# From which slice on a second weight-conversion step is allowed: slice 18 or slice 13

## The chip, the cores and the metric

One core of a Trainium2 chip runs the whole program. The metric is the device time of one execution in microseconds (us). TensorE does the matrix products (PE in the profile, PEld its weight loads), VectorE is DVE, ScalarE ACT, GpSimd POOL, and SyncE (SP) issues most DMAs.

## The reference

Three layers follow each other:

```
attn: q, k, v of (4 batches, 8 heads, 576, 64); heads 0-3 masked to a band of 32, heads 4-7 to a stride of 32
x = attn as (2304 tokens, 512)
h = x @ w_in                      # 512 -> 2048
x = (h * sigmoid(1.702 h)) @ w_out  # 2048 -> 512
logits = x @ w_gate + log1p(exp(x @ w_noise)) * noise   # 8 experts, best two of each token
out[token] += weight * (relu(x @ w1[e]) @ w2[e])        # 512 -> 1024 -> 512
```

All is in float32. The part that the change touches is the second layer, the two products with `w_in` and `w_out`.

## The kernel before, in words

The second layer works on 6 chunks of 384 tokens, and its 2048 hidden columns are cut into 16 weight slices of 128. A step of the main loop is one (chunk, slice) pair, and here it is called a slice and numbered by its place `i` in the list `seq`: slices 0 to 7 are the first half of chunk 0, slices 8 to 23 the sixteen of chunk 1 (the "second chunk"), slices 24 to 31 the second half of chunk 0, then chunks 2 to 5. So the weight slices 8 to 15 are used for the first time in slices 16 to 23.

For accuracy each float32 operand is held as a rounded `hi` part and a remainder `lo`, and each product is made of three: hi by hi, hi by lo, lo by hi. In slice i TensorE runs the first product of slice i (`m1_l1`, lines 426 to 428, twelve matmuls) and then the second product of slice i-1 (`m1_l2`, lines 450 to 452, nine matmuls). Between a slice's two products lies the activation: ACT's tanh (L431), DVE's L433, ACT's rounding to the hi part of g (L438), and DVE's subtraction to the lo part (L440). L450 and L451 read g's hi part, L452 its lo part; L450 and L452 read the hi part of the weights, L451 their lo part.

The weights come as int64 words that hold two float32 numbers, and must be converted first. A wide piece is half a weight slice, 512 columns (`area`), for weight slices 0 to 13; the last two slices come in narrow pieces of 256 columns (`raw`). Each weight slice's half 0 goes to the first product, half 1 to the second. A conversion step (`w_step`, `w_bits`) takes one wide piece or up to two narrow ones, with three operations on DVE for each piece (L387, L390, L394). A generator yields between them, so that the loop strews them among the other DVE work. Half a slice later `w_split` emits the piece's rounding on ACT (L361) and its remainder on POOL (L362), and issues the load of the next piece into the buffer that this frees. Four wide pieces are under way at any time, and two narrow ones; a narrow piece may be stepped only `LATE = 2` calls of `w_split` (one slice) after its load was issued.

Every slice has one step in its first half, beside its first product: L387 is then ahead of L433 in DVE's order, L390 and L394 between L433 and L440. The first chunk's slices with even i, and all slices from `SMALLS` on, have a second step, behind L440:

```
conv = w_step() if i < HALFC and not i % 2 or i >= SMALLS else iter(())
```

The orders of TensorE, ACT, DVE and POOL are as written out in the program up to the end of chunk 4 (`fine.close()`); after that only TensorE's order is, and the compiler's planner orders the others, as it does SP's queue all the time. Instructions of one engine start in order. The weight loads are chained to each other on SP's queue by `chained`.

Of the kernel before, what the change touches and what calls it, by code (L numbers as in the profile page):

```python
# [52 lines left out]
LATE = 2  # L53
REM = 1
HALFC = NFC // 2
SMALLS = 18
CONVAT = (4, 6, 8, 10, 12, 14)
WAIT1 = 15
R_PP = R_LG + 16 * TPC
# [40 lines left out]
def tile_kernel(ctx, tc, qkL, qkS, vL, vS, wm1, wm2, wgn, noise, cst, lst0, out):  # L100
# [19 lines left out]
    with ExitStack() as main, tc.manual_schedule(engines={mybir.EngineType.PE}):  # L120
# [236 lines left out]
        def w_split():  # L357

            for fc, s, w32, o, n in SPLIT.pop(0):
                hi, lo = W1[fc, s]  # L360
                nc.scalar.copy(hi[:, o:o + n], w32)  # L361
                nc.gpsimd.tensor_sub(lo[:, o:o + n], w32, hi[:, o:o + n].bitcast(F32))  # L362
                if n < 512:
                    held.pop()
                else:
                    w_raw(fc + 2, s)
            w_small()
            SPLIT.append([])
            done.append(0)

        def w_step():
            left = 512
            while PIECES and left:
                fc, s, raw, o, n = PIECES[0]
                if n < 512:
                    if len(done) < born[0] + LATE:
                        return
                    born.pop(0)
                PIECES.pop(0)
                left -= n  # L380
                yield from w_bits(fc, s, raw, o, n)
# [402 lines left out]
        for i, (c, fc) in enumerate(seq):  # L784
# [20 lines left out]
            w_split()  # L805
            conv = w_step() if i < HALFC and not i % 2 or i >= SMALLS else iter(())
            att.norms(conv)
# [219 lines left out]
```

## Time and profile before

| what | value |
|---|---|
| time, median of 3 runs | 1026.28 us (1025.94 to 1031.31) |
| the profiled execution's own time | 1025.36 us |
| its span, first to last instruction | 1023.6 us |
| TensorE busy | 991.5 us, 97% of the span |
| DVE / ACT / POOL busy | 48% / 39% / 22% |
| mean granted TensorE clock | 0.989 |

The profile is one execution on the chip. A busy time is the sum of an engine's instructions; in the timelines each row is one instruction or a run of equal ones, with its start, its duration, the engine, the line of the kernel, the operation, the tile written and the tiles read, and in brackets how long the engine was idle before it and what ended that. A releaser is inferred from semaphores. A matmul's end is modelled, so that consecutive ones overlap in the rows.

### The profile page before, as it was taken

To read this page: it belongs to the slowest core of one execution; us is meant where nothing else is said; L and a number is where in the kernel's file an instruction comes from. 1 tells how busy PE (TensorE), PEld (TensorE's weight loads), DVE (VectorE), ACT (ScalarE), POOL (GpSimd) and SP (SyncE) were. 2 spreads that over 40 slices of the span, in tenths; PEclk is the share of its full clock that TensorE was granted. 3 is DMA by queue.
4 is the path that set the end of the run, shared out by engine and by line. 5 is a ranking of instruction groups with operands and counts; after the bars stand their busy time and mean duration, and the time that the engine had idled before them with its cause. 6 is when DMAs were issued, how large, how long until landed. Compare 5 with 4: busy or idle time off the path is not lost. (4 is left out here: it accounts for less than half of the span.)

```text
span 1023.6 us, 16148 instructions
## 1 busy us (share of the span) xinstructions
PE 991.5 (97%) x5804; PEld 879.8 (86%) x5804; DVE 487.5 (48%) x1520; ACT 394.6 (39%) x1075; POOL 220.2 (22%) x206
## 2 busy tenths in 40 slices
PE   6899999999999999999999999999999999999996
PEld 5778898998888888899988889989999999999995
DVE  6979864547445544523655353342434243333310
ACT  5665533244444444323443242232424233332311
POOL 3565221112000200200320412050322205040303
PEclk9799999999999999999999999999999999999999
DMA  8835512022231325301342255262533527263403
GB/s 290 288 116 179 192 62 72 1 79 44 52 96 55 73 84 192 116 1 63 66 162 73 43 154 124 72 146 103 124 124 90 158 75 173 65 147 118 83 1 52
DMA packets 63393, 107.69 MB, mean 105 GB/s; under 512 B 12096, under 2 KB 25536, under 8 KB 63296
## 3 DMA queue, kind: packets, MB, share of 16 engines
q1 hardware_dynamic: 53104, 85.63, 26.5%
q0 software_dynamic: 10208, 21.02, 10.7%
q8 instruction: 46, 0.75, 0.3%
q14 instruction: 35, 0.29, 0.1%
HBM read 84.04 MB, written 22.73 MB: 104 GB/s over the span
## 5 line engine op out<-in xcount | busy, mean ns | idle before, releaser
L672 DVE SCALAR_TENSOR_TENSOR ht<-pb,ht 128x384 fp32r<-128x384 f32 (+1 forms) x128 | 62.5, 489 | 252.1 <-ACT ht L671 252.1
L671 ACT ACTIVATE ht<-pb 128x384 fp32r<-128x384 f32 (+1 forms) x128 | 56.0, 438 | 260.2 <-PE pb L670 259.2
L426 PE MATMUL pb<-xt,w 128*128 128x384 f32 x384 | 134.9, 351 | 0.0
L428 PE MATMUL pb<-xt,w 128*128 128x384 f32 x384 | 129.6, 337 | 0.0
L427 PE MATMUL pb<-xt,w 128*128 128x384 f32 x384 | 129.5, 337 | 0.0
L702 POOL DMA_INDIRECT out<-y,ix x40 | 64.9, 1623 | 295.0 <-ACT y L701 261.7
L685 PE MATMUL pb<-w,ht 128*128 128x512 f32 x320 | 127.8, 399 | 0.0
L686 PE MATMUL pb<-w,ht 128*128 128x512 f32 x320 | 125.4, 392 | 0.0
L687 PE MATMUL pb<-w,ht 128*128 128x512 f32 x320 | 125.2, 391 | 0.0
L450 PE MATMUL pb<-w,g 128*128 128x512 f32 x288 | 118.3, 411 | 1.8 <-ACT g L438 0.9
L433 DVE SCALAR_TENSOR_TENSOR th<-th,pb 128x384 f32<-128x384 f32 x96 | 53.0, 552 | 128.7 <-ACT th L431 128.6
L451 PE MATMUL pb<-w,g 128*128 128x512 f32 x288 | 113.4, 394 | 0.8 <-POOL w L362 0.8
L452 PE MATMUL pb<-w,g 128*128 128x512 f32 x288 | 114.0, 396 | 0.1
L575 POOL DMA_INDIRECT lst<-pay,si x36 | 36.0, 1001 | 342.6 <-DVE si L572 290.5
L593 DVE TENSOR_TENSOR w<-raw,w 128x512 fp32r<-128x512 f32 x128 | 83.8, 689 | 17.5 <-ACT w L592 17.5
L431 ACT ACTIVATE th<-pb 128x384 f32<-128x384 f32 x96 | 46.9, 489 | 111.4 <-PE pb L428 107.9
L668 PE MATMUL pb<-xa,w 128*128 128x384 f32 x256 | 87.3, 341 | 0.0
L670 PE MATMUL pb<-xa,w 128*128 128x384 f32 x256 | 86.4, 338 | 0.0
L669 PE MATMUL pb<-xa,w 128*128 128x384 f32 x256 | 86.0, 336 | 0.0
L592 ACT CAST w<-raw 128x512 fp32r<-128x512 f32 x128 | 73.8, 618 | 17.2 <-DMA raw<-wm 12.9
L438 ACT CAST g<-th 128x384 fp32r<-128x384 f32 x96 | 49.3, 513 | 75.9 <-DVE th L433 75.9
L426 PEld LDWEIGHTS pb<-xt,w 128*128 128x128 f32 x384 | 72.6, 189 | 2.5
(175 smaller groups left out, 1968.3 us busy)
## 6 DMA issues: line engine op xcount, KB each, us to landing
raw<-wm SPq DMA_DIRECT2D x136, 256.0 KB, 3.0
area<-wm SPq DMA_DIRECT2D x28, 512.0 KB, 4.3
out<-zero SPq DMA_DIRECT2D x7, 768.0 KB, 6.9
qk<-qkL SPq DMA_DIRECT2D x16, 304.0 KB, 3.4
att<-qkS SPq DMA_DIRECT2D x20, 189.0 KB, 4.9
qk<-qkS SPq DMA_DIRECT2D x20, 189.0 KB, 2.6
v<-vL SPq DMA_DIRECT2D x16, 192.0 KB, 3.1
att<-qkL SPq DMA_DIRECT2D x8, 304.0 KB, 6.0
```

The source lines that it names most:

```text
L426: nc.tensor.matmul(ps, w[0][:, a], X[c][:, 0, kc, :], start=(kc == 0), stop=False)
L427: nc.tensor.matmul(ps, w[0][:, a], X[c][:, 1, kc, :], start=False, stop=False)
L428: nc.tensor.matmul(ps, w[1][:, a], X[c][:, 0, kc, :], start=False, stop=(kc == 3))
L450: nc.tensor.matmul(o, g[:, 0, a], w[0], start=((c, fc) in FIRST), stop=False)
L451: nc.tensor.matmul(o, g[:, 0, a], w[1], start=False, stop=False)
L452: m = nc.tensor.matmul(o, g[:, 1, a], w[0], start=False, stop=((c, fc) in LAST))
L668: nc.tensor.matmul(ps, w[:, 0, a], x[:, 0, kc, :], start=(kc == 0), stop=False)
L669: nc.tensor.matmul(ps, w[:, 0, a], x[:, 1, kc, :], start=False, stop=False)
L670: nc.tensor.matmul(ps, w[:, 1, a], x[:, 0, kc, :], start=False, stop=(kc == 3))
L685: nc.tensor.matmul(o, g[:, 0, a], w[:, 0, 512:], start=(fc == 0), stop=False)
L686: nc.tensor.matmul(o, g[:, 0, a], w[:, 1, 512:], start=False, stop=False)
L687: m = nc.tensor.matmul(o, g[:, 1, a], w[:, 0, 512:], start=False, stop=(fc == NF2 - 1))
```

## The change

The constant `SMALLS` goes from 18 to 13. The line quoted above then allows a second step in slices 13 to 17 too: the sixth to the tenth slice of the second chunk. Nothing else changes.

```diff
-SMALLS = 18
+SMALLS = 13
```

## Rows read from the trace of the kernel before

**Rows 1.** The page's first part: busy us, share of the span, number of instructions.
```profile
PE 991.5 (97%) x5804; PEld 879.8 (86%) x5804; DVE 487.5 (48%) x1520; ACT 394.6 (39%) x1075; POOL 220.2 (22%) x206
```

**Rows 2.** Table by stretches, 150 to 200 us: length, busy by engine, clock, DMA.
```profile
150.00:200.00 50.00, 48.43 (x258) 43.10 (x257) 25.13 (x79) 15.76 (x36) 5.20 (x7) 1.00 0.15 47
```

**Rows 3.** Timeline of PE around slice 23's second product.
```profile
171.55 0.50 PE L450 MATMUL pb<-w,g 128*128 128x512 f32 x1 [0.81 <-ACT w L361]
172.81 0.50 PE L451 MATMUL pb<-w,g 128*128 128x512 f32 x1 [0.75 <-POOL w L362]
```

**Rows 4.** Timeline of DVE, 127 to 134 us: end of slice 13, slice 14, start of 15.
```profile
127.06 0.42 DVE L387 TENSOR_SCALAR cv<-area 128x512 int32<-128x512 int32 x1
129.33 0.56 DVE L433 SCALAR_TENSOR_TENSOR th<-th,pb 128x384 f32<-128x384 f32 x1 [1.85 <-ACT th L431]
129.81 0.68 DVE L390 SCALAR_TENSOR_TENSOR cv<-area,cv 128x512 int32<-128x512 int32 x1
130.59 0.69 DVE L394 SCALAR_TENSOR_TENSOR area<-area,cv 128x512 int32<-128x512 int32 x1
131.20 0.55 DVE L440 TENSOR_TENSOR g<-th,g 128x384 fp32r<-128x384 f32 x1
131.67 0.42 DVE L387 TENSOR_SCALAR cv<-area 128x512 int32<-128x512 int32 x1
133.52 0.56 DVE L433 SCALAR_TENSOR_TENSOR th<-th,pb 128x384 f32<-128x384 f32 x1 [1.43 <-ACT th L431]
```

**Rows 5.** Timeline of PE: first L450 and first L452 of slice 14's second product.
```profile
132.80 0.39 PE L450 MATMUL pb<-w,g 128*128 128x512 f32 x1
...
133.26 0.40 PE L452 MATMUL pb<-w,g 128*128 128x512 f32 x1
```

**Rows 6.** Timeline of POOL and ACT, 127 to 132 us.
```profile
127.42 1.28 POOL L362 TENSOR_TENSOR w<-area,w 128x512 fp32r<-128x512 f32 x1 [3.21 <-ACT w L361]
129.92 0.52 ACT L438 CAST g<-th 128x384 fp32r<-128x384 f32 x1 [0.62 <-DVE th L433]
131.32 0.62 ACT L361 CAST w<-area 128x512 fp32r<-128x512 f32 x1 [0.88 <-DVE area L394]
```

**Rows 7.** The page's DMA issues: the wide pieces, KB each, median us to landing.
```profile
area<-wm SPq DMA_DIRECT2D x28, 512.0 KB, 4.3
```

**Rows 8.** Timeline of DVE, a wide step's first two operations in slice 4.
```profile
78.18 0.43 DVE L387 TENSOR_SCALAR cv<-area 128x512 int32<-128x512 int32 x1
...
78.64 0.69 DVE L390 SCALAR_TENSOR_TENSOR cv<-area,cv 128x512 int32<-128x512 int32 x1
```

**Rows 9.** Timeline of POOL and DVE, 95 to 104 us.
```profile
95.77 3.17 POOL L362 TENSOR_TENSOR w<-area,w 128x512 fp32r<-128x512 f32 x2
98.17 1.32 DVE L390 SCALAR_TENSOR_TENSOR cv<-area,cv 128x512 int32<-128x512 int32 x1
...
102.44 1.28 POOL L362 TENSOR_TENSOR w<-area,w 128x512 fp32r<-128x512 f32 x1 [3.50 <-ACT w L361]
102.56 1.44 DVE L387 TENSOR_SCALAR cv<-area 128x512 int32<-128x512 int32 x1
```

**Rows 10.** Timeline of POOL, DVE and PE, 156 to 163 us: slices 20 and 21.
```profile
156.50 1.50 POOL L362 TENSOR_TENSOR w<-raw,w 128x256 fp32r<-128x256 f32 x2 [5.76 <-ACT w L361]
160.43 0.29 DVE L387 TENSOR_SCALAR cv<-raw 128x256 int32<-128x256 int32 x1 [3.72 <-DMA raw<-wm]
160.63 0.55 DVE L433 SCALAR_TENSOR_TENSOR th<-th,pb 128x384 f32<-128x384 f32 x1
161.96 0.55 DVE L440 TENSOR_TENSOR g<-th,g 128x384 fp32r<-128x384 f32 x1
162.57 0.50 PE L452 MATMUL pb<-w,g 128*128 128x512 f32 x1
```

**Rows 11.** Timeline of DVE, a narrow piece's three operations in slice 19.
```profile
151.94 0.29 DVE L387 TENSOR_SCALAR cv<-raw 128x256 int32<-128x256 int32 x1
152.27 0.43 DVE L390 SCALAR_TENSOR_TENSOR cv<-raw,cv 128x256 int32<-128x256 int32 x1
152.80 0.43 DVE L394 SCALAR_TENSOR_TENSOR raw<-raw,cv 128x256 int32<-128x256 int32 x1
```

## The prediction

> **What bounds the kernel now.** I read the page's busy line first, then the table by stretches, then the timelines of single engines. The reader is to see in the busy line that TensorE (PE) has 991.5 us of a span of 1023.6 [rows 1]: time comes or goes only where PE gets or loses an idle piece. The change acts in the second chunk (slices 8 to 23, counted from 0; "sixth slice of the second chunk" is slice 13), which ends near 173 us. In the stretch 150 to 200 PE is busy for 48.43 of 50 us at a granted clock of 1.00 [rows 2], so 1.57 us are lost there. PE's own timeline shows both pieces of that: 0.81 us before the first L450 of slice 23, released by ScalarE's cast L361, and 0.75 us before L451, released by GpSimd's subtract L362 [rows 3]. Slice 23 is the last of the sixteen weight slices to be used for the first time, and its last half was converted just too late. That is what the change can remove.
>
> What it can cost is read from VectorE (DVE). In a slice with one conversion step DVE runs L433, L390, L394, L440, then L387 of the next step, and then stands idle for 1.43 us of the 4.19 us from one L433 to the next [rows 4]. PE needs the hi half of g (ACT L438) for the first L450 of a slice's second product, and L440's result for the first L452, 0.46 us later; for slice 14 these stand at 132.80 and 133.26 [rows 5], where L440 ended at 131.75 [rows 4]. The margin is 1.05 + 0.46 = 1.51 us.
>
> **What moves.** No instruction is added or removed. Counting the pieces through the code: by slice 13's first half 24 wide pieces (512 columns) have been stepped, and 28 exist. Before, the last four go in the first halves of slices 14 to 17, and the eight narrow pieces (256 columns, two to a step) in 18 first half, 19 second, 21 first, 22 second. After, wide pieces go in 13 second half, 14 first and second, 15 first; the narrow pairs in 15 second half, 17 first, 18 second, 20 first. So the last pair comes 2.5 slices sooner, and slices 13, 14 and 15 carry two steps. With each piece move its three DVE operations, one ACT cast, one POOL subtract and its successor's load on SP. The loads are no limit for the wide pieces: a load goes out when the subtract of the piece four before is done, the last at 128.70 (127.42 + 1.28) [rows 6], and lands 4.3 us later [rows 7], about 133.0; it is needed after 136. Nothing of the attention is left on SP's queue there to be passed, so no other load is moved.
>
> **What goes.** The wait for slice 23's weights, 0.81 + 0.75 = 1.56 us [rows 3]: with the pair done 2.5 slices (10 us) sooner it goes entirely.
>
> **What comes.** A second wide step costs DVE 0.46 + 0.78 + 0.61 = 1.85 us of issue [rows 8, 4], against 1.43 idle. That alone is 0.4 us a slice and would be swallowed by the margin. But the subtract on POOL holds DVE up: L390, 0.68 us when undisturbed, took 1.32 and ended 0.55 after the pair of subtracts that began at 95.77 for 3.17; L387, normally 0.42, took 1.44 and ended 0.28 after the subtract 102.44 + 1.28 [rows 9, 4]. Today the subtract falls into DVE's idle time (127.42 after L387 at 127.06) [rows 6, 4]. With two steps there is no idle time left, and there are two subtracts of 1.28 a slice. The walk, in the clock of before:
>
> Slice 13. L387 of the new step at 127.06; the subtract 127.42 to 128.70 holds the new L390, which ends 128.70 + 0.55 = 129.25; L394 to 129.95; then L387 of slice 14's step, and L433 about 0.35 later (between 0.20 [rows 10] and its whole 0.42): 130.2 instead of 129.33.
>
> Slice 14. L390 130.7, L394 131.5, L440 132.1 to 132.6: within 133.26, no stall. The next L387 ends about 132.85, then the waiting subtract runs to 134.1, L390 ends 134.7, the second subtract, ready since 132.9, takes the gap before L394 and runs to 135.9, L394 ends 136.4; L433 of slice 15 at 136.7 instead of 133.52.
>
> Slice 15. L438 follows L433 by 0.59 and takes 0.52 [rows 4, 6]: done 137.8, where PE wants it at 132.80 + 4.19 = 136.99: stall 0.8. L440 ends 139.1, wanted at 138.25: 0.85. Then a narrow pair (two times 0.33 + 0.53 + 0.34, about 1.2 each [rows 11]) under two more subtracts: L433 of slice 16 at 143.4, L438 done 144.5, wanted at 141.2 + 1.65 = 142.85: 1.65, and L440 0.1.
>
> Slice 16 has no step, but the pair's subtracts end only there, the first about 145.75. From the end of a first subtract to the use of the piece that its buffer then loads is 160.43 - (156.50 + 0.75) = 3.2 us [rows 10]. In slice 17 that L387 stands ahead of L433: 148.9, L438 done 150.2, wanted at 148.75: 1.45, and L440 0.2. Before has this once, in slice 21: DVE idle 3.72 us for the load, L433 at 160.63, and the first L452, at 162.57, followed L440 closely [rows 10], so it was nearly free. After, it falls twice (slices 17 and 20), and the rounds feed each other through the same load, so slice 20 pays about 1.5 again, slices 18 and 19 together 0.4.
>
> Sum: 1.65 + 1.75 + 1.65 + 0.4 + 1.5 = 6.95 us. The same way of walking laid over slices 18 to 23 of before gives 1.9 us where the trace has 1.57; I take off that sixth: 5.8. Less 1.56: +4.2. From both sides: no subtract in the way gives -1.56 (with 0.4 us a slice within the margin); every operation held as above and POOL first each time gives about +7. I take +4.5, a little above the corrected walk, since the rows used lie close.
>
> One operation's hold is shown by no row here: L440 beside a subtract. By the rows of L390, which like it reads two tiles, it would be held. The Trainium skill, SBUF — State Buffer, section "Who interferes with whom", says that a DVE instruction with two SBUF inputs contends with a GpSimd instruction that reads SBUF, and that the one coming second is blocked for the whole of the other; the rows of L387 and L390 agree (0.28 and 0.55 us left after the subtract's end). By it the uncorrected sum stands; were L440 exempt, about 0.6 us of it would go.
>
> From the end of the second chunk PE is bound as before, so the loss stays to the end. The profiled execution took 1025.36, so 1029.9; the median shown is 0.92 above it, and I forecast on that scale: 1026.28 + 4.5 = 1030.8 us. A change under 0.5% (5.1 us) can't be told from none.
>
> **Rivals.** (a) The margin takes it: DVE's operations win the port often enough that L440 is never over 1.5 us late. Only the 1.56 us go: 1025.36 - 1.56 = 1023.8, or 1024.7 on the median's scale, not slower. For it: slices 8 to 11 had DVE held by 1 us a slice [rows 9], and PE stayed fed; against it: those slices are longer by their attention work and carry one step. Place: the first L450 of slices 15 and 16; it decides if L433 of slice 15 comes before about 135. 0.15. (b) The rounds compound: POOL goes first each time, slice 16 pays again, and each narrow round starts late: 3 us on top, +7.5, 1033.8. For it: one load loop of 3.2 us links all rounds; against: slice 16 and 19 first halves are free of steps. 0.13. (c) Instructions that the compiler orders itself (SP's queue, everything from the last chunk on) come in another order; no row prices that, so I take it as wide as my own walk, 6 us either way. That PE's order is written out throughout speaks against it. 0.10. That the second step finds no piece is ruled out by the loads above. (d) My forecast, +2.5 to +6.5: 0.62.
>
> **How the numbers follow.** (d)'s own range is 1028.8 to 1032.8; somewhat under two fifths of it lies over +5.1: same 0.38, slower 0.24. (a) same 0.15; (b) slower 0.13; (c) faster 0.04, same 0.03, slower 0.03. Faster 0.04, same 0.56, slower 0.40. The range 1026.0 to 1033.8 leaves out most of (a) and the ends of (c) and (b).
>
> **What would show it.** Right: no wait of PE for L361 or L362 in slice 23; PE waits for ACT g L438 and DVE g L440 in slices 15 to 17 and 20, 1 to 2 us each; L390 or L394 at 1.2 us or more between 127 and 143; PE busy lower by 4 to 6 us between 130 and 170. Wrong: PE idle for less than 2 us in that stretch, or differences that first appear after 175 us.

## The result, and the profile after

The change made the kernel slower: 1035.73 us median of 7 runs (1033.94 to 1037.64), against 1027.69 us for the kernel before in 7 runs beside them (1025.94 to 1031.31). The ratio is 1.0072, with a 95% interval of 1.0058 to 1.0085, so about +7.4 us (6.0 to 8.7). The profiled execution of after took 1037.64 us, with a span of 1035.9 and a mean clock of 0.985; that is the longest of its seven runs.

The busy line of the page after, against [rows 1]:

```profile
PE 997.8 (96%) x5804; PEld 882.0 (85%) x5804; DVE 492.8 (48%) x1520; ACT 394.1 (38%) x1075; POOL 221.8 (21%) x206
```

DVE has the same 1520 instructions and is busy 5.3 us longer, so some of them were held, that is, took longer than by themselves. The table by stretches says where PE lost (columns: length; busy and count for PE, PEld, DVE, ACT, POOL; clock; DMA share; GB/s). After:

```profile
130.00:150.00 20.00, 16.51 (x78) 13.41 (x77) 16.24 (x23) 6.41 (x13) 7.80 (x7) 1.00 0.17 58
150.00:175.00 25.00, 22.84 (x109) 18.95 (x108) 13.46 (x30) 7.57 (x17) 4.46 (x6) 1.00 0.19 60
```

The same stretches before:

```profile
130.00:150.00 20.00, 20.00 (x102) 18.22 (x101) 13.10 (x26) 7.85 (x16) 5.89 (x6) 1.00 0.16 54
150.00:175.00 25.00, 23.43 (x115) 20.36 (x114) 13.95 (x31) 8.43 (x20) 5.20 (x7) 1.00 0.20 62
```

Between 130 and 150 us PE goes from fully busy to 3.49 us idle. In the next stretch the old wait of [rows 3] is gone and others stand there. PE's waits after, 115 to 200 us (total, times, longest):

```profile
PE pb L450 <- ACT g L438: 3.3, 4, 1.1
PE pb L452 <- DVE g L440: 2.2, 2, 1.7
```

No wait for L361 or L362 is left. The six pieces on PE's timeline, in the second products of slices 14 (the first row that waits), 15 (two), 16, 17 and 20:

```profile
134.72 0.40 PE L451 MATMUL pb<-w,g 128*128 128x512 f32 x1
135.68 0.50 PE L452 MATMUL pb<-w,g 128*128 128x512 f32 x1 [0.56 <-DVE g L440]
136.01 0.40 PE L450 MATMUL pb<-w,g 128*128 128x512 f32 x1
...
140.46 0.50 PE L450 MATMUL pb<-w,g 128*128 128x512 f32 x1 [0.79 <-ACT g L438]
...
142.86 0.50 PE L452 MATMUL pb<-w,g 128*128 128x512 f32 x1 [1.67 <-DVE g L440]
...
147.32 0.50 PE L450 MATMUL pb<-w,g 128*128 128x512 f32 x1 [0.48 <-ACT g L438]
...
152.85 0.50 PE L450 MATMUL pb<-w,g 128*128 128x512 f32 x1 [0.94 <-ACT g L438]
...
167.50 0.50 PE L450 MATMUL pb<-w,g 128*128 128x512 f32 x1 [1.11 <-ACT g L438]
```

The bracket, the idle time ahead of an instruction, is not the whole loss. From L451 at 134.72 to L452 at 135.68 are 0.96 us, where undisturbed neighbours start 0.23 apart, as in [rows 5] (0.46 for two): 0.73 are lost, and the bracket says 0.56, because L451's modelled end counts as busy. The matmul behind it comes 0.33 later (136.01) instead of 0.23, another 0.10. So I count by starts. In slices 14 to 20 the starts lie 7.15 us further apart than undisturbed ones, and eleven matmuls that follow a pause cost 0.10 each: 8.3 us. By the same count the wait of [rows 3] cost 2.1 us, not 0.81 + 0.75 = 1.56; a slower matmul behind L452 at 162.57 [rows 10] makes it 2.2 for slices 18 to 23 of before. The net is +6.1, which a pair of rows confirms. The tenth and the 26th L433 (slices 9 and 25), in after:

```profile
105.61 0.54 DVE L433 SCALAR_TENSOR_TENSOR th<-th,pb 128x384 f32<-128x384 f32 x1
...
185.37 0.55 DVE L433 SCALAR_TENSOR_TENSOR th<-th,pb 128x384 f32<-128x384 f32 x1 [1.89 <-ACT th L431]
```

and in before:

```profile
103.92 0.54 DVE L433 SCALAR_TENSOR_TENSOR th<-th,pb 128x384 f32<-128x384 f32 x1
...
177.58 0.55 DVE L433 SCALAR_TENSOR_TENSOR th<-th,pb 128x384 f32<-128x384 f32 x1 [2.62 <-ACT th L431]
```

79.76 against 73.66 us: the change costs 6.1 us there. The two profiles differ by 12.3 us in all: 1.4 before the first slice, 0.3 up to slice 9, these 6.1, 2.1 between slices 25 and 60 (below), and 2.4 later, where in after the clock is 0.88 and 0.55 in the stretches 528 to 531 and 531 to 534 us.

How it happens is read from DVE and POOL, slices 13 to 17. DVE after:

```profile
129.21 1.73 DVE L390 SCALAR_TENSOR_TENSOR cv<-area,cv 128x512 int32<-128x512 int32 x1
...
132.11 0.55 DVE L433 SCALAR_TENSOR_TENSOR th<-th,pb 128x384 f32<-128x384 f32 x1
132.57 0.69 DVE L390 SCALAR_TENSOR_TENSOR cv<-area,cv 128x512 int32<-128x512 int32 x1
133.36 0.69 DVE L394 SCALAR_TENSOR_TENSOR area<-area,cv 128x512 int32<-128x512 int32 x1
133.97 1.65 DVE L440 TENSOR_TENSOR g<-th,g 128x384 fp32r<-128x384 f32 x1
135.55 1.51 DVE L387 TENSOR_SCALAR cv<-area 128x512 int32<-128x512 int32 x1
...
139.31 0.55 DVE L433 SCALAR_TENSOR_TENSOR th<-th,pb 128x384 f32<-128x384 f32 x1
...
141.17 1.63 DVE L440 TENSOR_TENSOR g<-th,g 128x384 fp32r<-128x384 f32 x1
142.72 1.37 DVE L387 TENSOR_SCALAR cv<-raw 128x256 int32<-128x256 int32 x1
...
151.49 0.29 DVE L387 TENSOR_SCALAR cv<-raw 128x256 int32<-128x256 int32 x1 [3.63 <-DMA raw<-wm]
```

POOL after:

```profile
129.10 1.29 POOL L362 TENSOR_TENSOR w<-area,w 128x512 fp32r<-128x512 f32 x1 [3.21 <-ACT w L361]
133.80 2.97 POOL L362 TENSOR_TENSOR w<-area,w 128x512 fp32r<-128x512 f32 x2 [3.41 <-ACT w L361]
141.01 2.94 POOL L362 TENSOR_TENSOR w<-area,w 128x512 fp32r<-128x512 f32 x2 [4.23 <-ACT w L361]
```

In slices 14 and 15 POOL begins a pair of subtracts just before L440 is up. L440 takes 1.65 and 1.63 us where it took 0.55 [rows 4], then the second subtract holds L387 (1.51 and 1.37). The delay reaches the next L433: 139.31 - 132.11 = 7.20 us, where 4.19 is undisturbed [rows 4]. The last row is the round of the narrow pieces: DVE waits 3.63 us for the load, as in [rows 10], and the L433 behind it comes at 151.70, so that PE waits, up to 152.85.

### The profile page after: what moved, and what is told of

It reads as the page before. It is cut to its first block, busy times and chain, and to the rows that moved or that the text cites. A ratio compares the mean times of both kernels' runs of the same rounds, so it can differ in the third digit from the quotient of the medians.

```text
span 1035.9 us, 16147 instructions
## 1 busy us (share of the span) xinstructions
PE 997.8 (96%) x5804; PEld 882.0 (85%) x5804; DVE 492.8 (48%) x1520; ACT 394.1 (38%) x1075; POOL 221.8 (21%) x206
## 5 line engine op out<-in xcount | busy, mean ns | idle before, releaser
L450 PE MATMUL pb<-w,g 128*128 128x512 f32 x288 | 119.1, 414 | 5.1 <-ACT g L438 4.9
L452 PE MATMUL pb<-w,g 128*128 128x512 f32 x288 | 114.9, 399 | 2.4 <-DVE g L440 2.2
L451 PE MATMUL pb<-w,g 128*128 128x512 f32 x288 | 113.7, 395 | 0.0
L433 DVE SCALAR_TENSOR_TENSOR th<-th,pb 128x384 f32<-128x384 f32 x96 | 52.9, 552 | 126.2 <-ACT th L431 119.6
L438 ACT CAST g<-th 128x384 fp32r<-128x384 f32 x96 | 49.3, 513 | 85.2 <-DVE th L433 85.1
```

The costliest lines, as they stand in the source:

```text
L450: nc.tensor.matmul(o, g[:, 0, a], w[0], start=((c, fc) in FIRST), stop=False)
L451: nc.tensor.matmul(o, g[:, 0, a], w[1], start=False, stop=False)
L452: m = nc.tensor.matmul(o, g[:, 1, a], w[0], start=False, stop=((c, fc) in LAST))
```

## The experiments

My theory: the loss is DVE's two wide steps in slices 13 to 15, held by POOL's subtracts (slices 14 to 16), plus the narrow pieces' load rounds (slices 17 to 20). Rivals: the DVE work alone, the earlier narrow steps alone, and something later or elsewhere in the program. Each result is given first as the ratio to the time of the kernel before in runs beside it, with the 95% interval, then as the change of the second chunk in that run's profile, counted as above from the tenth to the 26th L433.

**1. The changed kernel again** (no edit).

> The changed kernel once more, unaltered. In its first profile PE waits 7.1 us for g in slices 14 to 20 (4.9 for ACT L438, 2.2 for DVE L440), its tanh products come 6.1 us later by the end of the second chunk than in the kernel before (7.79 at slice 25 against 1.69 at slice 12), and the span is 12.3 us longer; 1.4 us lie before slice 0 and 4.4 us after slice 25. Theory 1 (the loss is made in the second chunk, the rest is scatter from run to run): the 6.1 us come again within 0.7, the 1.4 and the 4.4 don't, and the time is 6 to 8 us over the kernel before. Rival (a cost that is made later in the program as well): 3 us or more lie after slice 25 again, at the same slices (38, 55, 88 to 93).

1.0077 (1.0061 to 1.0092). The second chunk costs +6.9 in this profile, 0.8 more than in the first (I had allowed 0.7), with the same waits up to slice 16; in slice 17 the wait grew, and the granted clock fell behind it. Of the 4.4 us behind slice 25, which I had put down to scatter, 2.7 came again, 1.9 of them in the two waits treated below the table of all runs. PE and the table by stretches of this run:

```profile
152.26 0.50 PE L450 MATMUL pb<-w,g 128*128 128x512 f32 x1 [1.60 <-ACT g L438]
```

```profile
152.00:155.00 3.00, 2.69 (x7) 1.87 (x8) 2.35 (x5) 0.98 (x4) 0.74 (x1) 0.70 0.03 12
155.00:158.00 3.00, 3.00 (x13) 2.71 (x13) 1.83 (x5) 0.93 (x3) 0.73 (x1) 0.73 0.49 135
158.00:161.00 3.00, 3.00 (x16) 2.61 (x15) 1.95 (x5) 0.75 (x2) 0.00 (x0) 1.00 0.07 27
```

0.70 and 0.73 are means over stretches partly at the lower of the two levels (1.2 GHz) and partly at the upper (2.4). The profile of after has no such dip between 130 and 175, though its wait of 1.67 is longer.

**2. Second steps from slice 16 on.**

```diff
-SMALLS = 13
+SMALLS = 16
```

> SMALLS = 16: one wide piece is stepped as second step (slice 16) instead of three and a narrow pair in a row (slices 13 to 15); the last narrow pair is still two half slices sooner than before. Theory 1 (the loss comes from consecutive slices with two steps): no PE wait over 0.5 us in slices 13 to 18, the wait of 1.56 us in slice 23 gone, up to 1.5 us of waits in slice 20 for a load ahead of L433; time within 1.5 us of the kernel before. Rival (moving the narrow pairs forward is what costs): 3 us or more slower than before.

1.0006 (0.9995 to 1.0018), second chunk +1.1. The pauses of slices 14 to 16 are gone; PE waits for L438 twice, 1.16 and 0.20 us, in slices 20 and 22:

```profile
PE pb L450 <- ACT g L438: 1.4, 2, 1.2
```

So the second steps of slices 13 to 15 carry most of the loss.

**3. Narrow pieces may be stepped only three half slices after their load was issued** (otherwise as changed).

```diff
-LATE = 2
+LATE = 3
```

> SMALLS = 13 as in the changed kernel, but LATE = 3: the narrow pairs after the first go in second halves (slices 17, 19, 21) instead of 17 first, 18 second, 20 first, so that no L433 stands behind an L387 that waits for its load. Theory 1 with its load rounds: the waits of slices 14 to 16 stay (about 3.5 to 4 us), those of slices 17 and 20 (0.48 + 0.94 + 1.11 us by the profile after) fall by 1.5 us or more; time 1.5 to 2.5 us below the changed kernel. Rival (the rounds cost nothing, the port does all): same as the changed kernel within 0.7 us.

1.0027 (1.0013 to 1.0042), second chunk +3.2. PE's waits, 115 to 200 us, and the table by stretches:

```profile
PE pb L452 <- DVE g L440: 2.2, 2, 1.7
PE pb L450 <- ACT g L438: 0.8, 1, 0.8
```

```profile
143.00:146.00 3.00, 3.00 (x10) 2.71 (x9) 2.47 (x7) 0.32 (x1) 0.00 (x0) 0.50 0.00 0
```

Slices 14 and 15 wait as in after, slices 17 and 20 no longer: these were the load rounds. The time is 3.2 us under that of experiment 1 by the medians and 5.1 by the ratios, more than the 1.5 to 2.5 that I had expected from the brackets. Behind the wait of 1.66 that ends at 141.76 the clock is 0.50, the lower level, for a whole stretch of 3 us. The first L450 of slices 15 and 16 in this run:

```profile
139.37 0.50 PE L450 MATMUL pb<-w,g 128*128 128x512 f32 x1 [0.79 <-ACT g L438]
...
147.15 0.40 PE L450 MATMUL pb<-w,g 128*128 128x512 f32 x1
```

Slice 16's wait, 0.48 in after, is gone too: the slower products came after g was ready.

**4. No subtract in the way.** For the six wide pieces of weight slices 11 to 13 POOL writes zeros instead of subtracting, so the lo part of these weights is left out. The edit shifts later lines by 3 (L443 is L440).

```diff
-nc.gpsimd.tensor_sub(lo[:, o:o + n], w32, hi[:, o:o + n].bitcast(F32))
+if n == 512 and fc >= 11:
+    nc.gpsimd.memset(lo.bitcast(F32)[:, o:o + n], 0.0)
+else:
+    nc.gpsimd.tensor_sub(lo[:, o:o + n], w32, hi[:, o:o + n].bitcast(F32))
```

> SMALLS = 13, but for the wide pieces of weight slices 11 to 13 POOL writes zeros (a memset) instead of subtracting, so the lo part of these weights is left out; DVE's and ACT's work, the order and the loads stay. Theory 1 (a subtract on POOL that reads SBUF holds DVE's two-input operations and L387): L390 and L394 stay at 0.7 us between 127 and 143 us, the PE waits of slices 14 to 16 (about 4 us) fall below 1, those of slices 17 to 20 to about 2 at most; time 3.5 to 5.5 us below the changed kernel. Rival (DVE simply has too much to do in slices 13 to 15, whatever POOL does): the waits of slices 14 to 16 stay over 3 us and the time within 1 us of the changed kernel.

1.0005 (0.9993 to 1.0016), second chunk +0.8. That is 5.5 us under experiment 1 by the medians and 7.4 by the ratios, where I had expected 3.5 to 5.5. Writing zeros waits for no conversion, so all six ran early, and POOL did nothing from 123 to 140. POOL, then DVE, in this run:

```profile
120.06 2.86 POOL L363 MEMSET w<- 128x512 f32 x6
```

```profile
131.64 0.55 DVE L443 TENSOR_TENSOR g<-th,g 128x384 fp32r<-128x384 f32 x1
...
136.16 0.55 DVE L443 TENSOR_TENSOR g<-th,g 128x384 fp32r<-128x384 f32 x1
```

DVE issues the same two steps a slice, L440 is back at 0.55, and PE has no pause in slices 14 to 16. The rival that DVE's own work is too much falls. What is left are two waits for L438 of 0.28 and 1.04 us, in slices 17 and 20.

**5. The kernel before again** (no edit).

> The kernel before once more, unaltered, for a second profile of it. Theory 1: its first profile was one of its fastest executions (1025.36 us against 1028 to 1033 in 24 later ones); here PE waits about 1.8 us at L264 between 240 and 360 us and the products of slices 38 and 55 come 0.7 us later each, as in all profiles taken since, so that this part of the 12.3 us between the two first spans is not the change's. Rival: the waits at L264 are absent again, so the change shifts something into that stretch.

0.9998 (0.9985 to 1.0012). The second chunk is as in the first profile (+0.05). What I had expected of the later waits, told below, did not come: its profile has none.

**6. The wide pieces alone.** Second steps only in slices 13, 14 and 15, narrow pieces held to slice 18 as before.

```diff
-if len(done) < born[0] + LATE:
+if i < 18 or len(done) < born[0] + LATE:
...
-conv = w_step() if i < HALFC and not i % 2 or i >= SMALLS else iter(())
+conv = w_step() if i < HALFC and not i % 2 or i in (13, 14, 15) or i >= 18 else iter(())
```

> Only the wide half of the change: second steps in slices 13 and 14 (and, idle, 15), the narrow pairs held back to slices 18 first, 19 second, 21 first, 22 second as in the kernel before. Theory 1: the gaps at L440 and L438 of slices 14 to 16 come (0.7 + 0.95 + about 1, with one step less in slice 15), the 2 us at slice 23 stay; time 2 to 3.5 us over the kernel before, some 4 to 5 below the changed kernel. Rival (the narrow pairs cost nothing of their own): within 1.5 us of the changed kernel.

1.0056 (1.0038 to 1.0073), +5.8 us where I expected 2 to 3.5, and the second chunk costs +7.0. The pauses of slices 14 and 15 are those of after (0.56, 0.78 and 1.66 us in brackets), and slice 23's wait is back on PE's timeline:

```profile
177.02 0.50 PE L450 MATMUL pb<-w,g 128*128 128x512 f32 x1 [0.78 <-ACT w L361]
178.28 0.50 PE L451 MATMUL pb<-w,g 128*128 128x512 f32 x1 [0.75 <-POOL w L362]
```

The wide steps alone cost the changed kernel's pauses in slices 14 and 15, and without the earlier narrow steps nothing is given back. What I had not counted is the clock: 0.83 and 0.61 in the two stretches of 3 us from 140 on, and a second dip behind slice 23's waits (0.58 and 0.85 in the two from 179 on). The expectation's rival, narrow steps that cost nothing, asked for a time within 1.5 us of the changed kernel; it is 1.6 to 2.1 under, so the time alone does not decide, and experiment 3's timeline has to.

**7. From slice 16 on, and a narrow step of a first half begins only behind L440**, so that no L387 waiting for a load stands ahead of L433 (`early` takes `conv`'s place ahead of L440).

```diff
-SMALLS = 13
+SMALLS = 16
...
+narrow = bool(PIECES) and PIECES[0][4] < 512
+early = iter(()) if narrow else conv
-t, g = m1_l1(c, fc, step, conv)
+t, g = m1_l1(c, fc, step, early)
...
-next(conv, None)
+next(early, None)
...
-next(conv, None)
+next(early, None)
```

> SMALLS = 16, and a narrow step that falls in a slice's first half starts behind L440 instead of ahead of L433, so that no L433 waits for a narrow load. Theory 1: neither two-step overload nor a load ahead of L433 is left, and the last pair is done two half slices before it is needed, so the 2.0 us of slice 23 go and nothing comes: 1.5 to 2 us under the kernel before. Rival (the subtracts of narrow pieces still hold L440, or DVE waits in order for the load and makes the next L433 late): same as before within 0.7 us.

1.0003 (0.9990 to 1.0017), second chunk +1.3. Missed: PE waits for L438 four times:

```profile
PE pb L450 <- ACT g L438: 1.9, 4, 0.7
```

I read it as the narrow operations, moved behind L440, crowding the next L433; no run separates that.

**8. Experiments 3 and 4 together** (the lo part left out as in 4).

> The changed kernel with both suspected costs taken out: zeros written by POOL instead of the subtract for the wide pieces of weight slices 11 to 13 (their lo part is left out), and LATE = 3. Theory 1 closes: no PE gap over 0.5 us from slice 13 to 23, the 2 us of slice 23 gone, time 1.5 to 2.2 us under the kernel before. Rival (a third cost of the second steps, such as ACT's casts ahead of tanh): 1 us or more of gaps stay and the time is not under the kernel before.

0.9972 (0.9959 to 0.9984), -2.9 us; second chunk -2.2. PE, by stretches:

```profile
130.00:143.00 13.00, 13.00 (x66) 11.75 (x65) 9.83 (x20) 6.39 (x13) 1.50 (x2) 1.00 0.21 66
...
150.00:175.00 25.00, 25.00 (x127) 22.69 (x126) 11.69 (x25) 8.20 (x19) 3.11 (x5) 1.00 0.19 63
```

With the wide pieces' subtracts and the load rounds both out of the way, PE has no pause there, between 143 and 150 us neither, and what remains is the gain that the change was able to bring: the 2.2 us of slices 18 to 23, nearly all of them slice 23's.

**9 and 10. The wide second steps apart from each other**, all work done, `LATE = 3`, in slices 12 and 14 (9) or 11 and 13 (10).

```diff
-LATE = 2
+LATE = 3
...
-SMALLS = 13
+SMALLS = 15
...
-conv = w_step() if i < HALFC and not i % 2 or i >= SMALLS else iter(())
+conv = w_step() if i < HALFC and not i % 2 or i in (12, 14) or i >= SMALLS else iter(())
```

> A version meant to keep the gain without the cost, with all work done: second wide steps in slices 12 and 14 only (not in consecutive slices), narrow pairs by LATE = 3 in the second halves of slices 15, 17, 19 and 21. Theory 1 (a lone second wide step makes L433 late by about 1 us, which the margin of 1.5 us swallows, as in the run with SMALLS = 16; two in a row don't fit): gaps of PE in slices 12 to 23 under 0.8 us in all, the 2.0 us of slice 23 gone, 1 to 2 us under the kernel before. Rival (a wide second step in slice 14 and a narrow pair in slice 15 are already too close): gaps of 1.5 us or more in slices 14 to 16, and the kernel before is not beaten.

> The same with the second wide steps in slices 11 and 13, so that the narrow pair in slice 15 has a one-step slice ahead of it; slice 11 still has attention work on DVE. Theory 1: gaps under 0.8 us in all, 1 to 2 us under the kernel before, as with slices 12 and 14 or better by up to 0.5. Rival (attention's DVE work beside two steps in slice 11 delays L440 or the attention products): a new gap of 1 us or more in slices 11 to 13 and no gain over the kernel before.

0.9999 (0.9988 to 1.0011) and 1.0009 (0.9995 to 1.0023), second chunk +1.3 and 0.0. Both missed the 1 to 2 us under before that I had expected. A single pair of subtracts is enough to hold L440. DVE, POOL and PE of experiment 10:

```profile
133.65 1.62 DVE L440 TENSOR_TENSOR g<-th,g 128x384 fp32r<-128x384 f32 x1
```

```profile
133.49 2.94 POOL L362 TENSOR_TENSOR w<-area,w 128x512 fp32r<-128x512 f32 x2 [3.41 <-ACT w L361]
```

```profile
135.33 0.50 PE L452 MATMUL pb<-w,g 128*128 128x512 f32 x1 [1.57 <-DVE g L440]
```

This one wait, 1.73 by starts, eats most of the gain of slice 23.

**11 and 12. Wide pieces are split only in the second half of a slice**, to put the subtracts behind L440: on the changed kernel (11) and on experiment 10 (12).

```diff
-def w_split():
+def w_split(hold=False):
+if hold:
+    SPLIT[1][:0] = [x for x in SPLIT[0] if x[4] == 512]
+    SPLIT[0] = [x for x in SPLIT[0] if x[4] < 512]
...
-w_split()
+w_split(i >= HALFC)
```

> The changed kernel (SMALLS = 13), but the cast and the subtract of a wide piece stepped in a slice's second half wait for the next slice's second half, so that no wide subtract starts beside L394 and L440; both subtracts of a two-step slice then fall behind L440, together. Theory 1 in its sharper form (what costs most is L440 held by a subtract: 1.65 and 1.63 us instead of 0.55): the gaps at L452 (0.73 and 1.83) fall under 0.5 together; L433 still comes late, so gaps at L450 of 1 to 3 us stay in slices 15 to 17; time 1 to 3 us under the changed kernel. Rival (only the total of subtracts matters, wherever they fall): the sum of the gaps of slices 14 to 17 stays at 4 us or more and the time within 1 us of the changed kernel.

> The same hold on the version with second wide steps in slices 11 and 13 and LATE = 3, where one gap was left: 1.73 us at L452, behind an L440 of 1.62 us. Theory 1: that gap goes, gaps of slices 12 to 23 under 0.6 us in all, 1 to 2 us under the kernel before (0.1 to 0.2%). Rival: the held subtracts delay L433 instead, a gap of 1 us or more at an L450 takes its place, and the kernel before is not beaten.

1.0049 (1.0033 to 1.0065) and 0.9996 (0.9980 to 1.0011). Both missed, since the edit moved nothing that matters: in 11 the pairs of subtracts still start at 133.63 and 140.82 (133.80 and 141.01 in after), and PE waits in the same places. In after's own order ACT has nothing between the two casts of slice 14 (L361 at 133.11 and 134.09), so a later place in the program is no later start. In 12 L440's wait is there (1.67), and the clock behind it is 0.55 from 137 to 140. So 11 serves in effect as a third run of the changed kernel (second chunk +6.8).

**All runs beside each other**, in us against the kernel before: the second chunk from tenth to 26th L433, the same difference from the 26th to the 61st, and the measured difference, which is the ratio's excess over 1 times the median of before (the medians themselves differ by 8.0 us for after and by 6.4 for experiment 1).

| run | second chunk | 26th to 61st | measured (95%) |
|---|---|---|---|
| after | +6.1 | +2.1 | +7.4 (6.0 to 8.7) |
| 1 after again | +6.9 | +1.9 | +7.9 (6.3 to 9.5) |
| 2 from slice 16 | +1.1 | +1.9 | +0.6 (-0.5 to 1.9) |
| 3 LATE = 3 | +3.2 | +1.9 | +2.8 (1.3 to 4.3) |
| 4 zeros | +0.8 | +1.9 | +0.5 (-0.7 to 1.6) |
| 5 before again | 0.0 | 0.0 | -0.2 (-1.5 to 1.2) |
| 6 wide alone | +7.0 | 0.0 | +5.8 (3.9 to 7.5) |
| 7 narrow behind L440 | +1.3 | 0.0 | +0.3 (-1.0 to 1.7) |
| 8 zeros, LATE = 3 | -2.2 | 0.0 | -2.9 (-4.2 to -1.6) |
| 9 slices 12, 14 | +1.3 | +1.8 | -0.1 (-1.2 to 1.1) |
| 10 slices 11, 13 | 0.0 | +1.9 | +0.9 (-0.5 to 2.4) |
| 11 after, held | +6.8 | +1.9 | +5.1 (3.4 to 6.7) |
| 12 as 10, held | +1.7 | +1.9 | -0.4 (-2.1 to 1.1) |

The second chunk alone lies within the measured interval in ten of thirteen, and at most 0.6 us outside it. The second column comes from two waits of about 1 us, slices 38 and 55. The first of them on PE's timeline after:

```profile
262.00 0.44 PE L264 MATMUL pb<-pt,v 126*64 126x126 f32 x4 [0.98 <-ACT pt L242]
```

The profiles of after and of experiments 1 to 4 and 9 to 12 have them, those of before and of 5 to 8 have not. The split goes with the chip: experiments 1 to 4 ran on one, 5 to 8 on a second, 9 to 12 on a third; on which before and after were profiled the record does not say. Adding that column makes six of the nine runs that have it come out above their interval, so the times don't bear it out as a cost against before. Whether the timed executions of before have the waits as well on the first and third chip no trace shows, and why L242 starts late is not settled.

None of the versions that do the full work beats before.

## Why the prediction was wrong

The direction and the place were right; 1035.73 us lies above the range (to 1033.8), and against a median of before that was itself 1.4 higher than the one shown, the difference of +7.4 us is above +4.5 and outside forecast (d)'s +2.5 to +6.5. On the forecast's own scale, 1026.28 + 7.4 = 1033.7 would lie just inside the range, at the end that rival (b) gave it.

**What goes.** Right: slice 23's wait vanishes. Sized by its brackets at 1.56; by starts it is 2.1, or 2.2 for slices 18 to 23, and experiment 8 gains 2.2.

**Slice 13.** Right: L390 is held to 0.55 us past the subtract's end (129.10 + 1.29 + 0.55 = 130.94 = 129.21 + 1.73).

**Slice 14.** Wrong: I let L440 come ahead of the waiting subtract, without a stall. POOL came first, 133.80 against 133.97, because the cast of the piece before had ended at 133.73 while L394 was still running. PE lost 0.73 there, and L433 of slice 15 came about 0.9 later than my walk has it (139.31 against 136.7 + 1.7, the start that after already has on slice 9). That much of rival (b), POOL first each time, is what happened; its own addition, a slice 16 that pays again, did not come. Its figure, +7.5, is the nearest to the measured +7.4, but by luck: the profile's second chunk gives +6.1, without that addition.

**L440 beside a subtract.** No row of before showed it. Here it took 1.65 and 1.63 us instead of 0.55: held until the first subtract of the pair ended, and done 0.41 us after it (135.62 against 135.21, 142.80 against 142.38). The rule that I cited from the Trainium skill, SBUF — State Buffer, section "Who interferes with whom" (a DVE instruction with two SBUF inputs against a GpSimd instruction that reads SBUF), agrees, and so does experiment 4, where no subtract is there and L440 takes 0.55. Of the two rows that the prediction set beside that sentence only L390's belongs to it: L387 reads one tile, and was held here all the same (1.51 and 1.37 us instead of 0.42 and 0.29).

**Slices 15 to 20.** Lost between starts, after, beside my walk: slice 15 0.95 + 1.84 (1.65), slice 16 0.64 (1.75), slice 17 1.11 + 0.22 (1.65), slices 18 and 19 0.17 (0.4), slice 20 1.26 + 0.23 (1.5). With slice 14's 0.73 that is 7.15; the walk has 6.95. Slice by slice it erred, and that the sum held is luck: slices 14 and 15 cost 1.87 more than walked, slices 16 to 20 1.67 less. With the slower matmuls behind the pauses, which the walk leaves out, the loss is 8.3. Experiment 3 confirms slices 17 and 20 as load rounds, and experiment 4, which keeps the narrow steps and their subtracts, slices 14 to 16 as the wide pieces' subtracts.

**The step that failed** is "I take off that sixth: 5.8", with the +4.5 taken from it. The walk over slices 18 to 23 of before gave 1.9, and I called it too long because two idle brackets add up to 1.57. By starts, and with the slower matmul behind each pause, that stretch lost 2.2: the walk was about a seventh too short. Set right the other way, 6.95 x 2.2 / 1.9 = 8.0, less 2.2, gives +5.8, against +6.1 in this profile. I scaled a sum that was already short with a wrong yardstick: a loss of 5.8 where the profile has 8.3, and a gain of 1.56 where it has 2.2. 8.3 less 2.2 is the profile's +6.1; the rest up to the measured +7.4 stays open. The interval begins at 6.0, and three profiles of the changed kernel (after, 1, 11) give +6.1, +6.9 and +6.8 beside measured +7.4, +7.9 and +5.1.

**A term that was not in the sum** is the clock. In the profiles of experiments 1, 3, 6, 11 and 12 the granted clock falls for about 3 us behind waits of 1.5 to 1.7 us. Experiments 3 and 6 show its price: from the first L450 of slice 15 to that of slice 16 took 6.86 us in after, without a dip, and 7.78 with one, 0.9 more, although slice 16's wait (0.64 by starts) stands in the first figure and not in the second. How many of the timed executions had a dip no trace shows.

**Rivals.** (a), the margin takes it, falls: it was to decide at L433 of slice 15, before about 135, and that came at 139.31. (c), another order by the compiler, is not needed for the second chunk; whether the waits from slice 38 on belong to it or to the chip is open. "Wrong if differences first appear after 175 us": they appear at 135. The sign on PE's busy time, 4 to 6 us less between 130 and 170, came as well: 34.35 us instead of 40.00.

## What to carry to other kernels

An idle slot on one engine may be no room for work when its operations read memory beside another engine's: here the slot that the second step filled was the one in which POOL's subtract had run unnoticed, and the subtract moved onto the one operation that TensorE waits for. Measure a stall from start to start and include the slower instruction behind it; a check of a model against idle brackets corrected the sum in the wrong direction. A second step paid here only with both of its followers out of the way, the subtract and the reload, as experiment 8 shows.

## What I had not expected of the hardware

The granted clock fell behind a TensorE pause of 1.60 us in slice 17 of experiment 1, and not behind one of 1.66 in slice 15 of the same execution; in experiment 3 it fell to 0.50 behind the pause of slice 15 (1.66), and in after, with 1.67 there, it stayed at 1.00. So the same pause had this price in some executions and not in others; what decides it no run here shows.

POOL's zero fill of a 128x512 tile took about 0.5 us (2.86 for six), against 1.28 for the subtract of the same size [rows 6].
